# Grouped-query decode attention with adaLN and a small MLP: coarser K turns, 1/L folded into the gather, masks on GpSimd, two more looped V halves, fewer filler matmuls

## The chip, the core and the metric

The kernel runs on one core of one Trainium2 chip. The metric is device time in microseconds (us). The kernel before takes 354.18 us, the median of three runs that lie between 354.14 and 354.19. A profile of one further execution is read throughout. Its engines are PE (TensorE matmuls; PEld is the loading of their weights), DVE (VectorE), ACT (ScalarE), POOL (GpSimd) and SP (SyncE, which here only issues DMAs). A small q behind an engine's name means its sequencer.

## What is computed

One token passes an adaLN block: modulation from a condition vector, a layer norm, attention over a cache of 32768 positions with 8 KV heads and 4 query heads on each, an output projection, a second layer norm and a ReLU MLP.

```python
mod = (_silu(c) @ w_mod).reshape(c.shape[0], 6, 1, -1)
...
h = _layernorm(x, axis=-1) * (1 + ca) + sa
x = x + ga * _A_ref(h, A_k_cache, A_v_cache, A_wq, A_wo)
h = _layernorm(x, axis=-1) * (1 + cb) + sb
x = x + gb * _B_ref(h, B_w1, B_w2)
```

`_A_ref` projects h to q, takes softmax(q·K / sqrt(128))·V for each head and multiplies by `wo`; `_B_ref` is `relu(x @ w1) @ w2`. Everything is bfloat16. K and V of one KV head are 8.39 MB each (32768 x 128), so 134 MB of the 149.4 MB that the kernel reads are the cache.

## The kernel before

**The stream.** SP issues nearly all loads, in one fixed order (the list `stream`, L161 to L168). A load is issued when the code first needs it (`need`, L171), together with everything that stands before it in the list. SP takes its instructions in order: a load that waits holds back all loads behind it. The order is: K of head 0 in two halves with `w_mod` and `wq` between them; then K of head g+1 and V of head g, for g from 0 to 5; then the last head's K mixed with V of head 6; then V of head 7, `wo`, `w1` and `w2`. A whole K or V is one transfer of 8.39 MB. From `HALVED` = 5 on, transfers are halves of 4.19 MB: K6a, K6b, V5a, V5b, K7a, V6a, K7b, V6b, and V7 as one half and two quarters.

**The ring.** All these tiles live in a pool `ring` of three slots of 64 KB per partition. A tile takes the slot of the tile that came three before it, so its first load waits for the last reader of that tile. K6 takes the slot of V3, V5 that of K5, K7 that of V4, V6 that of K6, V7 that of V5, and the tile of the tail weights (`tail_sb`) that of K7.

**One head.** K arrives with 256 positions on each partition, as four tiles u of 64 positions. `turn_k` (L429) lets DVE turn half a tile, 128 x 2048 float32, in place by 32 x 32 blocks. `scores` (L448) multiplies that half with block-diagonal queries (`qbd`, built by ACT in `build_qbd`, L410): 8 matmuls of 512 columns for each half tile, 64 for a head, summed into two PSUM banks. `softmax` (L466) is a generator. Its steps are the maximum (DVE), a transpose of it (PE), the row maximum (DVE), the exponential (ACT, which also sums L), the turn of P (DVE), and 1/L by a matmul and a reciprocal. `pv` (L512) is 64 matmuls of 512 columns for a head, which add four blocks of P·V into 16 PSUM rows. `blocks` (L544) masks and gathers these rows with DVE, `o_cols` turns the result with a matmul, `normalise` (L562) multiplies by 1/L and writes a masked form `oA`, `spread` and `project` (L578, L589) apply `wo`.

**Loops.** `pv` comes in two forms. Unrolled, every matmul names its slice of V. As a loop (L525 to L531) the body of four matmuls stands once, in a section `tc.tile_critical()`, and a register that PE counts up gives the place of the slice in P and in V. Before the section PE waits for everything that was emitted ahead of it, and behind it PE's sequencer counts up a semaphore by which others know that the loop is over. Before the change V0 to V4 and V5b run as loops, the rest unrolled.

**Order.** PE and DVE take the order in which the code emits their work (`manual_schedule`, L633). For each head g the loop at L643 emits: turns and scores of K(g+1), the softmax of head g+1 up to the turn of P, and `pv(g)` within it. For g = 5 `pv(5, (0, 1))`, the use of V5a, stands directly behind the scores of K6 (L655), ahead of that softmax, and V5b behind it (L665). The last two heads are written out from L671 on: turns and scores of K7a, `pv(6, (0, 1))` (L687), turns and scores of K7b, the rest of V6 and V7, then the tail.

**Tail.** Parts of `wo` with index below `WOROWS` are multiplied with the vector as the stationary side (one row of 512 columns a matmul), the others with the weights stationary (four matmuls of one column for each). `keep_clock(n)` (L626) issues n matmuls of 512 columns into a bank that nobody reads.

Of the kernel before, what the change touches and what calls it, by code (L numbers as in the profile page):

```python
# [17 lines left out]
def kernel(  # L18
# [15 lines left out]
    P = 128  # L34
# [12 lines left out]
    WOP = [(0, Hkv // 2), (Hkv // 2, Hkv // 4), (Hkv - 2, 1), (Hkv - 1, 1)]  # L47
    WOROWS = 2
    LAST = Hkv - 1
# [28 lines left out]
    front = ctx.enter_context(tc.tile_pool(name="front", bufs=1))  # L78
    mask4 = front.tile([P, 32], F32, name="mask4_sb")[:, 0:REP]
    ring = ctx.enter_context(tc.tile_pool(name="ring", bufs=3))  # L80
# [124 lines left out]
    nc.vector.tensor_reduce(  # L205
        out=mask4, in_=ident_f[:].rearrange("p (x q) -> p q x", q=REP), op=ALU.add, axis=AX.X,
    )

    cmask, rsel = {}, {}
    for n in sorted({n * REP for _, n in WOP}):  # L210
        cmask[n] = const.tile([P, P // n], F32, name=f"cmask{n}")
        nc.vector.tensor_reduce(
            out=cmask[n][:], in_=ident_f[:].rearrange("p (c r) -> p c r", r=n), op=ALU.add, axis=AX.X,
        )
        rsel_f = const.tile([P, n], F32, name=f"rsel_f{n}")
        nc.vector.tensor_reduce(
            out=rsel_f[:], in_=ident_f[:].rearrange("p (c r) -> p r c", r=n), op=ALU.add, axis=AX.X,
        )
        rsel[n] = const.tile([P, n], BF16, name=f"rsel{n}")
        nc.vector.tensor_copy(out=rsel[n][:], in_=rsel_f[:])  # L220

# [4 lines left out]
    qsel = mask4[0:16, :]  # L226
    oT_sb = const.tile([P, Hq], BF16)
    oA = [const.tile([P, n * REP, P // (n * REP)], BF16, name=f"oA{i}") for i, (_, n) in enumerate(WOP)]
# [31 lines left out]

    acc_ps = ps_acc.tile([P, REP + KT], F32)
    nc.vector.memset(acc_ps[:], 0.0)
    oT_ps, attnT_ps = acc_ps[:, 0:REP], acc_ps[:, REP:REP + KT]

# [63 lines left out]
    for u in range(2):  # L328
        for half in range(2):
            t = need(("k", 0, u))[:, 32 * half:32 * half + 32, :].rearrange("p j d -> p (j d)").bitcast(F32)  # L330
            nc.vector.transpose(out=t, in_=t)  # L331

    mod_b = two_banks("mod_ps")
    mod_ps = [row_bank(mod_b[:, i, :]) for i in range(2)]
    to_rows(mod_ps, siluT, wm_sb, 6)
# [51 lines left out]
    q_b = two_banks("q_ps")  # L387
    q_ps = [row_bank(q_b[:, i, :]) for i in range(2)]
    wq_f = wq_sb.rearrange("p kt (i h a e) -> p kt i a h e", i=2, a=4, e=32)
# [20 lines left out]
    def build_qbd(g):  # L410
        d_ap = qbd[g % 2][:]
        d_ps = d_ap.ap[0][0]
        s_ap = qrep_sb[:]
        s_ps = s_ap.ap[0][0]
        for a in range(4):
            o = AP(d_ap.tensor, d_ap.offset + (32 * a) * d_ps + 4 * 7 + 32 * a,
                   [[d_ps, 32], [QW, 4], [1, 4]])
            i = AP(s_ap.tensor, s_ap.offset + (32 * a) * s_ps + REP * g,
                   [[s_ps, 32], [Hq, 4], [1, 4]])
            nc.scalar.copy(out=o, in_=i)  # L420


    S_tiles, m_tiles, S_ps_tiles = {}, {}, {}
    PT_tiles, Linv_tiles = {}, {}
# [4 lines left out]
    def turn_k(g, u, half):  # L429

        if u == 0 and half == 0:
            S_tiles[g] = two_banks("S_ps")
            m_tiles[g] = spool.tile([P, NG], F32, tag="m2", name="m2")
# [5 lines left out]
        t = nc.vector.transpose(out=KTt.bitcast(F32), in_=KTt.bitcast(F32))  # L439
        behind_loop(t)  # L440
# [21 lines left out]

    def bank_max(g, G):
        behind_loop(nc.vector.reduce_max(out=m_tiles[g][:, G:G + 1], in_=S_tiles[g][:, G, :], axis=AX.X))

    def softmax(g):  # L466

        S_g, m2 = S_tiles.pop(g), m_tiles.pop(g)
        m_p = spool.tile([P, 1], F32, tag="m_p", name="m_p")
        if g < LAST:  # L470
            behind_loop(nc.vector.reduce_max(out=m_p[:], in_=S_g.rearrange("p g f -> p (g f)"), axis=AX.X))  # L471
        else:
            nc.vector.reduce_max(out=m_p[:], in_=m2[:], axis=AX.X)
        yield
# [33 lines left out]
        Linv = spool.tile([P, REP], F32, tag="Linv", name="Linv", bufs=3)  # L508
        nc.vector.reciprocal(out=Linv[:], in_=L_ps[:])  # L509
        Linv_tiles[g] = Linv  # L510

    def pv(g, us, js=range(16)):  # L512

        nb = 4 // len(us)

        PT_g = PT_tiles[g][:].rearrange("p (h j c) -> p h (j c)", h=2, c=32)
        Vs = [need(("v", g, u)) for u in us]

        def step(u, V, PT, Vx):
            nc.tensor.matmul(o_tiles[g][:], lhsT=PT, rhs=Vx, start=False, stop=False, skip_group_check=True)  # L520

        Vf = [V.rearrange("p (s j) d -> p s (j d)", s=4) for V in Vs]
        if g < HALVED or g == HALVED and us[0] > 0:

            with tc.tile_critical() as section:  # L525
                last_loop[:] = loop[:] = [section.name]
                with nc.tensor.Fori(0, 512 - 32 * nb + 1, 32 * nb) as at:
                    for b in range(nb):
                        for u, V in zip(us, Vf):
                            step(u, V, PT_g[:, u // 2, 32 * b + 16 * (u % 2):][:, bass.DynSlice(at, 16)],  # L530
                                 V[:, :, Dh * b:][:, :, bass.DynSlice(at * (Dh // 32), Dh)])  # L531
        else:
            for u, V in zip(us, Vf):
                for j in js:
                    c0 = 32 * j + 16 * (u % 2)
                    step(u, V, PT_g[:, u // 2, c0:c0 + 16], V[:, :, Dh * j:Dh * (j + 1)])

    def open_o(g):
        o_tiles[g] = ps_o.tile([16, 4 * Dh], F32, tag="o", name="o_ps")
        nc.vector.memset(o_tiles[g][:], 0.0)  # L540

    Y_tiles = {}

    def blocks(g):  # L544

        o = o_tiles.pop(g)[:].rearrange("p (s d) -> p s d", s=4)
        Y = spool.tile([16, Dh], F32, tag="Y", name="Y", bufs=1)
        nc.vector.tensor_tensor(  # L548
            out=o, in0=o, in1=smask[:].unsqueeze(2).to_broadcast([16, 4, Dh]), op=ALU.mult,
        )  # L550
# [3 lines left out]
    def o_cols(g):  # L554
        nc.tensor.matmul(  # L555
            oT_ps, lhsT=Y_tiles.pop(g)[:], rhs=qsel, start=True, stop=True, skip_group_check=True,
        )
# [4 lines left out]
    def normalise(g):  # L562
# [3 lines left out]
        CH = P // (n * REP)  # L566
        o_g = oT_sb[:, REP * g:REP * (g + 1)]
        nc.vector.tensor_tensor(out=o_g, in0=oT_ps, in1=Linv_tiles.pop(g)[:], op=ALU.mult)
        nc.vector.tensor_tensor(
            out=oA[i][:, REP * (g - g0):REP * (g - g0 + 1), :],  # L570
            in0=o_g.unsqueeze(2).to_broadcast([P, REP, CH]),
            in1=cmask[n * REP][:].unsqueeze(1).to_broadcast([P, REP, CH]), op=ALU.mult,
        )
        PT_tiles.pop(g)
# [58 lines left out]
    with tc.manual_schedule(engines={mybir.EngineType.PE, mybir.EngineType.DVE}):  # L633
# [189 lines left out]
```

## Time and profile before

| quantity | value |
|---|---|
| time, median of 3 runs | 354.18 us |
| span of the profiled execution, first to last instruction | 352.6 us |
| difference of the two, around the span | 1.6 us |
| PE busy, share of the span | 79% |
| DVE busy | 57% |
| ACT, POOL busy | 7%, 1% |
| matmul instructions | 1310 |
| mean granted clock of TensorE, of full speed | 0.937 |
| bytes moved, mean rate | 149.59 MB, 424 GB/s |

A row of the timeline gives start and length in us, engine, line, operation, what is written and read, the shape and the count; in brackets stands the idle time of the engine before it and what ended it. Consecutive instructions of one line are one row. `SPq ... DMA_DIRECT2D` is the issue of a load, not its transfer. A transfer's landing is seen where an engine's idle time ends by it.

### The profile page before, as it was taken

Reading aid. Unit: us, or ns where it says so; the run is one execution under the profiler, and the core shown is the slowest. Engines: PE = TensorE matmul, PEld = TensorE weight load, DVE = VectorE, ACT = ScalarE, POOL = GpSimd, SP = SyncE. Lnnn points to the kernel's source line nnn. Section 1 sums busy time; section 2 is a strip of 40 time slices with the busy share of each in tenths; the row PEclk is TensorE's granted clock in tenths of the full one; section 3 lists DMA queues with packets and bytes.
Section 4 is the critical chain, followed back from the end, with each engine's and each line's share of the span. In section 5 each row is a group of like instructions: output and inputs, shape, how many; then the busy total and the mean of one; then the engine's idle time right before and its main releaser. Section 6 shows DMA issues by size and latency. Waiting matters only on the chain. (4 is left out here: it accounts for less than half of the span.)

```text
span 352.6 us, 3715 instructions
## 1 busy us (share of the span) xinstructions
PE 277.9 (79%) x1310; PEld 113.5 (32%) x1310; DVE 201.0 (57%) x226; ACT 25.1 (7%) x69; POOL 3.1 (1%) x15
## 2 busy tenths in 40 slices
PE   0065891895998599976998499968999799989994
PEld 0021330331333234322333134323444233434442
DVE  6663564984079614974099506975684257744142
ACT  1200103002000200001000200011000100011000
POOL 2000000000000000000000000000000000000000
PEclk9999897798999879998999879996999989999999
DMA  9999989999999999999999999999999999999995
GB/s 357 398 435 452 472 388 461 454 394 454 461 394 448 439 424 439 424 433 439 416 446 446 409 440 461 411 394 454 431 414 435 457 417 420 444 439 409 425 425 214
DMA packets 5224, 149.59 MB, mean 424 GB/s; under 512 B 604, under 2 KB 988, under 8 KB 1628
## 3 DMA queue, kind: packets, MB, share of 16 engines
q1 hardware_dynamic: 5180, 149.43, 98.5%
q8 instruction: 8, 0.13, 0.1%
q14 instruction: 4, 0.03, 0.0%
q10 hardware_dynamic: 32, 0.00, 0.0%
HBM read 149.42 MB, written 0.00 MB: 424 GB/s over the span
## 5 line engine op out<-in xcount | busy, mean ns | idle before, releaser
L439 DVE STREAM_TRANSPOSE Ksb<-Ksb 128x2048 f32<-128x2048 f32 x60 | 133.1, 2276 | 60.2 <-DMA Ksb<-in_A_k_cache_dram 60.2
L520 PE MATMUL o_ps<-Vsb,P_g 128*16 (+1 forms) x512 | 127.0, 408 | 13.0 <-ACT P_g L495 10.0
L458 PE MATMUL S_ps<-Ksb,qbd 128*128 128x512 bf16 x512 | 120.4, 386 | 10.9 <-DVE Ksb L439 9.3
L458 PEld LDWEIGHTS <-qbd 128*128 128x128 bf16 x512 | 49.6, 98 | 78.1 <-issue 21.8
L520 PEld LDWEIGHTS o_ps<-Vsb,P_g 128*16 x352 | 34.0, 97 | 67.8 <-issue 36.5
L520 PEld LDWEIGHTS <-P_g 128*16 128x16 bf16 x160 | 13.8, 90 | 19.0 <-issue 0.4
L420 ACT COPY qbd<-qrep_sb 32x16 bf16<-32x16 bf16 x32 | 6.4, 201 | 175.2 <-PE S_ps L458 174.1
L500 DVE STREAM_TRANSPOSE P_g<-P_g 128x1024 bf16<-128x1024 bf16 x8 | 10.0, 1245 | 14.1 <-ACT P_g L495 14.1
L471 DVE TENSOR_REDUCE m_p<-S_ps 128x1 f32<-128x1024 f32 x7 | 8.6, 1223 | 13.3 <-PE S_ps L458 13.3
L322 PE MATMUL mod_ps<-wmq_sb,siluT 128*1 128x512 bf16 x24 | 3.6, 624 | 9.9 <-DMA wmq_sb<-in_w_mod_dram 9.9
L331 DVE STREAM_TRANSPOSE Ksb<-Ksb 128x2048 f32<-128x2048 f32 x4 | 8.9, 2280 | 1.6 <-DMA Ksb<-in_A_k_cache_dram 1.6
L476 PE MATMUL mT_ps<-ident_f,m_p 128*1 128x128 f32 x8 | 2.2, 270 | 8.9 <-DVE m_p L471 7.9
L495 ACT ACTIVATE P_g<-S_ps,nbias 128x1024 bf16<-128x1024 f32 x8 | 8.9, 1114 | 0.2
L506 PE MATMUL L_ps<-Lexp,ones_f 128*128 128x4 f32 x16 | 3.1, 263 | 6.3 <-DVE Lexp L503 4.3
L492 ACT ACTIVATE nbias<-Mb_ps 128x1 f32<-128x1 f32 x8 | 1.4, 171 | 88.3 <-PE Mb_ps L490 88.3
L509 DVE RECIPROCAL Linv<-L_ps 128x4 f32<-128x4 f32 x8 | 1.3, 164 | 10.9 <-PE L_ps L506 10.9
L252 PE MATMUL xc_ps<-cx_sel,wmq_sb 16*128 16x2 bf16 x4 | 0.3, 172 | 8.7 <-DVE wmq_sb L246 8.7
L555 PE MATMUL acc_ps<-mask_sb,Y 16*128 16x4 f32 x16 | 3.0, 258 | 4.9 <-DVE Y L551 4.9
L548 DVE TENSOR_TENSOR o_ps<-o_ps,smask 16x512 f32<-16x512 f32 x8 | 5.3, 668 | 2.8 <-PE o_ps L520 2.8
L586 DVE CAST o_sb<-o_ps 128x4 bf16<-128x4 f32 (+2 forms) x4 | 0.7, 165 | 10.3 <-PE o_ps L582 10.3
L506 PEld LDWEIGHTS L_ps<-Lexp,ones_f 128*128 128x128 f32 x16 | 2.6, 203 | 9.6 <-issue 5.6
L551 DVE TENSOR_REDUCE Y<-o_ps 16x128 f32<-16x512 f32 x8 | 5.4, 678 | 0.3
(116 smaller groups left out, 82.8 us busy)
## 6 DMA issues: line engine op xcount, KB each, us to landing
Ksb<-in_A_k_cache_dram SPq DMA_DIRECT2D x5, 4096.0 KB, 23.5
Vsb<-in_A_v_cache_dram SPq DMA_DIRECT2D x5, 4096.0 KB, 38.0
wmq_sb<-in_A_wq_dram SPq DMA_DIRECT2D x1, 4096.0 KB, 28.0
Vsb<-in_A_v_cache_dram SPq DMA_DIRECT2D x2, 2048.0 KB, 38.1
Ksb<-in_A_k_cache_dram SPq DMA_DIRECT2D x1, 4032.0 KB, 37.1
wmq_sb<-in_w_mod_dram SPq DMA_DIRECT2D x1, 3072.0 KB, 18.8
tail_sb<-in_A_wo_dram SPq DMA_DIRECT2D x1, 2048.0 KB, 23.0
tail_sb<-in_B_w_dram SPq DMA_DIRECT2D x1, 1792.0 KB, 30.4
```

Of the source, the lines that this page charges most:

```text
L322: nc.tensor.matmul(dst[j // 4][32 * (j % 4):32 * (j % 4) + 1, :], lhsT=src_T[:, kt:kt + 1], rhs=w[:, kt, j * 512:(j + 1) * 512], start=(kt ...
L331: nc.vector.transpose(out=t, in_=t)
L420: nc.scalar.copy(out=o, in_=i)
L439: t = nc.vector.transpose(out=KTt.bitcast(F32), in_=KTt.bitcast(F32))
L458: nc.tensor.matmul(S_ps_tiles[g], lhsT=qbd[g % 2][:, hp, 4 * (7 - s):4 * (7 - s) + P], rhs=KTv[:, 16 * sl:16 * sl + 16, h, :, par], start= ...
L471: behind_loop(nc.vector.reduce_max(out=m_p[:], in_=S_g.rearrange("p g f -> p (g f)"), axis=AX.X))
L495: nc.scalar.activation(out=P_g[:], in_=S_g.rearrange("p g f -> p (g f)"), func=ACT.Exp, bias=nbias[:], scale=scale, accum_out=l_g[:],)
L500: behind_loop(nc.vector.transpose(out=P_g[:], in_=P_g[:]))
L506: nc.tensor.matmul(L_ps[:], lhsT=ones_f[:], rhs=Lexp[:], start=True, stop=True)
L520: nc.tensor.matmul(o_tiles[g][:], lhsT=PT, rhs=Vx, start=False, stop=False, skip_group_check=True)
L548: nc.vector.tensor_tensor(out=o, in0=o, in1=smask[:].unsqueeze(2).to_broadcast([16, 4, Dh]), op=ALU.mult,)
L551: nc.vector.tensor_reduce(out=Y[:], in_=o.rearrange("p s d -> p d s"), op=ALU.add, axis=AX.X)
```

## The change

The parts, in the order of the program:

- the front builds its masks with fewer instructions, `rsel` is cast by GpSimd, and the two zeroed PSUM banks of `mod_ps` and `q_ps` are one memset each;
- `build_qbd`: one masked GpSimd multiply per head in place of four ACT copies;
- `turn_k`: one turn of a whole tile (128 x 4096 float32) in place of two of half a tile, also for the first half of K0;
- `softmax`: the last head takes its maximum in one pass like the others; L is summed per row block by one matmul with `mask16`, and 1/L is a 16 x 1 column;
- `blocks` multiplies by 1/L while it masks, all heads' columns of o stay in one PSUM tile, and `normalise` writes `oA` once for a part of `wo`;
- `pv`: V5a and V6a become loops, so that with V0 to V4 and V5b eight loops run in place of six; unrolled, head 7's first matmul opens its bank and saves a memset;
- the tail: the third part of `wo` goes with rows (`WOROWS` 3), and 13 of the 18 filler matmuls are gone.

```diff
-    WOROWS = 2
+    WOROWS = 3
...
-    for hp in range(4):
-        h, par = hp // 2, hp % 2
-        src = AP(ib.tensor, ib.offset + 64 * h + par, [[ib.ap[0][0], P], [0, 4], [2, 32]])
-        nc.vector.tensor_copy(out=sel[:, hp, :].rearrange("p (a c) -> p a c", a=4), in_=src)
+    nc.vector.tensor_copy(
+        out=sel.rearrange("p (h par) (a c) -> p h par a c", h=2, a=4),
+        in_=AP(ib.tensor, ib.offset, [ib.ap[0], [64, 2], [1, 2], [0, 4], [2, 32]]),
+    )
...
     def build_qbd(g):
-        for a in range(4):
-            o = AP(d_ap.tensor, d_ap.offset + (32 * a) * d_ps + 4 * 7 + 32 * a,
-                   [[d_ps, 32], [QW, 4], [1, 4]])
...
-            nc.scalar.copy(out=o, in_=i)
+        d_ap, s_ap, m_ap = qbd[g % 2][:], qrep_sb[:], rowpick[:]
+        nc.gpsimd.tensor_tensor(
+            out=AP(d_ap.tensor, d_ap.offset + 4 * 7, [d_ap.ap[0], [QW, 4], [32, 4], [1, 4]]),
+            in0=AP(s_ap.tensor, s_ap.offset + REP * g, [s_ap.ap[0], [Hq, 4], [0, 4], [1, 4]]),
+            in1=AP(m_ap.tensor, m_ap.offset + OUT0, [m_ap.ap[0], [0, 4], [1, 4], [0, 4]]),
+            op=ALU.mult,
+        )
...
     def turn_k(g, u, half):
...
         if g == 0 and u < 2:
             return
+        if half:
+            return
+        KTt = Ksb.rearrange("p j d -> p (j d)")
         t = nc.vector.transpose(out=KTt.bitcast(F32), in_=KTt.bitcast(F32))
         behind_loop(t)
...
-        Lexp = spool.tile([P, REP], F32, tag="Lexp", name="Lexp")
-        nc.vector.tensor_scalar(out=Lexp[:], in0=mask4, scalar1=l_g[:], scalar2=None, op0=ALU.mult)
         yield
-        L_ps = small_ps([P, REP], "L_ps")
-        nc.tensor.matmul(L_ps[:], lhsT=ones_f[:], rhs=Lexp[:], start=True, stop=True)
+        L_ps = small_ps([16, 1], "L_ps")
+        nc.tensor.matmul(L_ps[:], lhsT=mask16, rhs=l_g[:], start=True, stop=True)
...
+    def looped(g, us):
+        return g <= HALVED or g == LOOPED and us == (0, 1)
+
     def pv(g, us, js=range(16)):
...
-        if g < HALVED or g == HALVED and us[0] > 0:
+        if looped(g, us):
...
     def blocks(g):
...
-        nc.vector.tensor_tensor(
-            out=o, in0=o, in1=smask[:].unsqueeze(2).to_broadcast([16, 4, Dh]), op=ALU.mult,
+        nc.vector.scalar_tensor_tensor(
+            out=o, in0=o, scalar=Linv_tiles.pop(g)[:], in1=smask[:].unsqueeze(2).to_broadcast([16, 4, Dh]),
+            op0=ALU.mult, op1=ALU.mult,
         )
...
     def normalise(g):
...
-        nc.vector.tensor_tensor(out=o_g, in0=oT_ps, in1=Linv_tiles.pop(g)[:], op=ALU.mult)
...
+        if g == g0 + n - 1:
+            nc.vector.tensor_tensor(
+                out=oA[i][:], in0=oT_ps[:, REP * g0:REP * (g0 + n)].unsqueeze(2).to_broadcast([P, n * REP, CH]),
+                in1=cmask[n * REP][:].unsqueeze(1).to_broadcast([P, n * REP, CH]), op=ALU.mult,
+            )
...
-        bank_max(h, 0)
         pv(g, (0, 1))
...
-        bank_max(h, 1)
         soft = softmax(h)
...
         project(0)
-        keep_clock(2)
         o_cols(LAST)
-        keep_clock(2)
         project(1)
         normalise(LAST)
         spread(3)
-        keep_clock(2)
         project(2)
-        keep_clock(1)
         join_rows()
         keep_clock(1)
         project(3)
...
-            keep_clock(2)
             x1_ps.append(four_rows(e, "x1"))
             keep_clock(2)
 
-        keep_clock(3)
         layernorm_T(x1T[:], stat2, h2T[:], modT_sb[:, 3 * KT:4 * KT], ncb[:], "ln2", meanwhile)
...
-        keep_clock(3)
+        keep_clock(2)
```

In the built program the loads keep their order. Two of them have a new wait: the second halves of V5 and of V6 now stand behind the end of the loop that reads the first half (counts 18 and 24 of the semaphore that PE's sequencer raises by 3 for each loop). The place of a loop's slice lies in a register, so the planner takes the loop to read all of its V tile, and both halves are written to one tile.

More of the change, by code (lines that the diff above doesn't have):

```diff
@@ L78 @@
     front = ctx.enter_context(tc.tile_pool(name="front", bufs=1))
-    mask4 = front.tile([P, 32], F32, name="mask4_sb")[:, 0:REP]
+    mask16 = front.tile([P, 32], F32, name="mask16_sb")[:, 0:16]
+    mask4 = mask16[:, 0:REP]
     ring = ctx.enter_context(tc.tile_pool(name="ring", bufs=3))
@@ L205 @@
     nc.vector.tensor_reduce(
-        out=mask4, in_=ident_f[:].rearrange("p (x q) -> p q x", q=REP), op=ALU.add, axis=AX.X,
+        out=mask16.rearrange("p (s q) -> p s q", q=REP),
+        in_=AP(ident_f[:].tensor, ident_f[:].offset, [ident_f[:].ap[0], [0, 4], [1, REP], [REP, P // REP]]),
+        op=ALU.add, axis=AX.X,
     )
@@ L219 @@
         rsel[n] = const.tile([P, n], BF16, name=f"rsel{n}")
-        nc.vector.tensor_copy(out=rsel[n][:], in_=rsel_f[:])
+        nc.gpsimd.tensor_copy(out=rsel[n][:], in_=rsel_f[:])
     smask = const.tile([16, 4], F32)
@@ L258 @@
     cT, xT = xc[:, 0, :], xc[:, 1, :]
-    acc_ps = ps_acc.tile([P, REP + KT], F32)
+    acc_ps = ps_acc.tile([P, Hq + KT], F32)
     nc.vector.memset(acc_ps[:], 0.0)
-    oT_ps, attnT_ps = acc_ps[:, 0:REP], acc_ps[:, REP:REP + KT]
+    oT_ps, attnT_ps = acc_ps[:, 0:Hq], acc_ps[:, Hq:Hq + KT]
     def bank(name):
@@ L328 @@
     for u in range(2):
-        for half in range(2):
-            t = need(("k", 0, u))[:, 32 * half:32 * half + 32, :].rearrange("p j d -> p (j d)").bitcast(F32)
-            nc.vector.transpose(out=t, in_=t)
+        t = need(("k", 0, u)).rearrange("p j d -> p (j d)").bitcast(F32)
+        nc.vector.transpose(out=t, in_=t)
     mod_b = two_banks("mod_ps")
-    mod_ps = [row_bank(mod_b[:, i, :]) for i in range(2)]
+    row_bank(mod_b)
+    mod_ps = [mod_b[:, i, :] for i in range(2)]
     to_rows(mod_ps, siluT, wm_sb, 6)
@@ L387 @@
     q_b = two_banks("q_ps")
-    q_ps = [row_bank(q_b[:, i, :]) for i in range(2)]
+    row_bank(q_b)
+    q_ps = [q_b[:, i, :] for i in range(2)]
     wq_f = wq_sb.rearrange("p kt (i h a e) -> p kt i a h e", i=2, a=4, e=32)
@@ L410, in build_qbd @@
     def build_qbd(g):
[L411 to L414, printed above, removed]
-        for a in range(4):
-            o = AP(d_ap.tensor, d_ap.offset + (32 * a) * d_ps + 4 * 7 + 32 * a,
-                   [[d_ps, 32], [QW, 4], [1, 4]])
[L418 to L423, printed above, removed]
+        d_ap, s_ap, m_ap = qbd[g % 2][:], qrep_sb[:], rowpick[:]
[5 more added lines that the diff above has]
+        )
+    S_tiles, S_ps_tiles = {}, {}
     PT_tiles, Linv_tiles = {}, {}
@@ L517, in pv, with step @@
         Vs = [need(("v", g, u)) for u in us]
-        def step(u, V, PT, Vx):
-            nc.tensor.matmul(o_tiles[g][:], lhsT=PT, rhs=Vx, start=False, stop=False, skip_group_check=True)
+        def step(u, V, PT, Vx, first=False):
+            nc.tensor.matmul(o_tiles[g][:], lhsT=PT, rhs=Vx, start=first, stop=False, skip_group_check=True)
         Vf = [V.rearrange("p (s j) d -> p s (j d)", s=4) for V in Vs]
-        if g < HALVED or g == HALVED and us[0] > 0:
+        if looped(g, us):
             with tc.tile_critical() as section:
@@ L555, in o_cols @@
         nc.tensor.matmul(
-            oT_ps, lhsT=Y_tiles.pop(g)[:], rhs=qsel, start=True, stop=True, skip_group_check=True,
+            oT_ps[:, REP * g:REP * (g + 1)], lhsT=Y_tiles.pop(g)[:], rhs=qsel,
+            start=True, stop=True, skip_group_check=True,
         )
```

24 lines of the change are left out of this document (6 added, 18 removed).

## The prediction

> **What bounds the kernel now.** I read the page first, then the chain of waits in order of time, then the timeline of SP alone.
>
> ```profile
> span 352.6 us, 3715 instructions
> PE 277.9 (79%) x1310; PEld 113.5 (32%) x1310; DVE 201.0 (57%) x226; ACT 25.1 (7%) x69; POOL 3.1 (1%) x15
> ...
> DMA  9999989999999999999999999999999999999995
> ...
> q1 hardware_dynamic: 5180, 149.43, 98.5%
> q8 instruction: 8, 0.13, 0.1%
> q14 instruction: 4, 0.03, 0.0%
> ```
>
> No engine is full, but SP's queue keeps the 16 DMA engines busy for 98.5% of the span, and the DMA row shows no slice below 8 tenths except the last. The load stream bounds the kernel: work on an engine counts only if it makes a load late, or lies behind the last load. The chain ends that way:
>
> ```profile
> 313.39 25.04 DMA tail_sb<-in_A_wo_dram
> 338.42 0.02 issue
> 338.44 11.14 DMA tail_sb<-in_B_w_dram
> 349.58 0.04 issue
> 349.62 0.29 PE end_ps L784 x4
> ```
>
> The last load ends at 349.58, and 3.0 us follow it. So the question for each edit is whether it opens a gap in the stream. The reserve is the distance from the issue of a load to the landing of the load ahead of it. The issues around the change, and the landings that DVE waited for:
>
> ```profile
> 234.34 0.81 SPq L154 DMA_DIRECT2D Vsb<-in_A_v_cache_dram  x2
> 256.12 0.33 SPq L154 DMA_DIRECT2D Ksb<-in_A_k_cache_dram  x1
> 270.62 0.33 SPq L154 DMA_DIRECT2D Vsb<-in_A_v_cache_dram  x1
> 270.99 0.43 SPq L154 DMA_DIRECT2D Ksb<-in_A_k_cache_dram  x1
> 271.46 19.78 SPq L154 DMA_DIRECT2D Vsb<-in_A_v_cache_dram  x4
> ...
> 313.02 1.75 SPq L154 DMA_DIRECT2D tail_sb<-in_A_wo_dram  x4
> ```
>
> ```profile
> 243.75 8.89 DVE L439 STREAM_TRANSPOSE Ksb<-Ksb 128x2048 f32<-128x2048 f32 x4 [2.73 <-DMA Ksb<-in_A_k_cache_dram]
> ...
> 282.51 4.51 DVE L439 STREAM_TRANSPOSE Ksb<-Ksb 128x2048 f32<-128x2048 f32 x2 [0.46 <-DMA Ksb<-in_A_k_cache_dram]
> ...
> 302.15 8.89 DVE L439 STREAM_TRANSPOSE Ksb<-Ksb 128x2048 f32<-128x2048 f32 x4 [2.70 <-DMA Ksb<-in_A_k_cache_dram]
> ```
>
> K6a lands at 243.75 and K7a at 282.51, four half transfers later: 38.76 / 4 = 9.69 us each. Hence K6b lands at 253.4, V5a at 263.1, V5b at 272.8, V6a at 292.2, K7b at 302.1, V6b at 311.8. V5a and V5b are issued together at 234.34, K7a at 256.12, V6a and K7b at 270.6 to 271.0. The load ahead of K7a, V5b, lands 16.7 us after K7a's issue: a delay of a few us anywhere costs nothing, as long as loads are issued in pairs like this.
>
> **The change part by part: the loops.** V5b now waits until the loop on V5a is over. That loop cannot start before V5a has landed, at 263.1, and SP issues in order, so K7a, V6a and K7b wait behind V5b. When V5a has landed, nothing is queued. The gap lasts until PE has come to the loop, has run it, SP has issued V5b and its transfer has started.
>
> ```profile
> 238.86 0.19 ACT L495 ACTIVATION_READ_ACCUMULATOR P_g<-S_ps,nbias 128x1 f32 x1
> 239.65 16.31 PE L520 MATMUL o_ps<-Vsb,P_g 128*16 x64 [2.04 <-ACT P_g L495]
> ...
> 256.51 14.07 PE L458 MATMUL S_ps<-Ksb,qbd 128*128 128x512 bf16 x64
> ...
> 270.53 7.07 PE L520 MATMUL o_ps<-Vsb,P_g 128*16 128x512 bf16 x32
> ...
> 280.74 9.03 PE L520 MATMUL o_ps<-Vsb,P_g 128*16 x32 [2.10 <-DMA Ksb<-in_A_k_cache_dram]
> ```
>
> The scores of K6 keep PE until 256.51 + 14.07 = 270.58, whatever V5a does. The entry into a section takes 0.6 us: ACT's sum is there at 239.05, and the loop on V4 starts at 239.65. Unrolled, 32 matmuls take 7.07 us; I take this for the loop too, since PE comes hot from the scores (the upper end is the 9.03 us of the loop on V5b, which started after an idle stretch). SP's issue follows a loop's end closely: the loop on V4 ends at 255.96, K7a is issued at 256.12, 0.16 us later.
>
> What is a load worth that meets an empty queue? The trace has one, the first:
>
> ```profile
> 0.74 0.38 SPq L154 DMA_DIRECT2D Ksb<-in_A_k_cache_dram  x1
> ...
> 12.76 8.89 DVE L331 STREAM_TRANSPOSE Ksb<-Ksb 128x2048 f32<-128x2048 f32 x4 [1.63 <-DMA Ksb<-in_A_k_cache_dram]
> ```
>
> A half of the same size needs 12.0 us from issue to use. The ends are 9.69 us (no start-up at all) and 12.0 us; I take 12.0, the only row with an empty queue. The Trainium skill (DMA: Bandwidth & Descriptors, Anatomy of one DMA) gives a fixed 2.0 us plus bytes over 436 GB/s, fitted on the other issue path; an estimate from it for 4.19 MB is 11.6 us, and by it each gap below would be 0.4 us shorter, the total 376.4.
>
> **The turns of K** move the start of that loop. A whole tile turns in the time of its halves, but PE gets nothing of it before the end.
>
> ```profile
> 223.51 8.85 DVE L439 STREAM_TRANSPOSE Ksb<-Ksb 128x2048 f32<-128x2048 f32 x4
> ...
> 232.41 1.90 PE L458 MATMUL S_ps<-Ksb,qbd 128*128 128x512 bf16 x8 [0.30 <-DVE Ksb L439]
> ```
>
> ```profile
> L439 DVE STREAM_TRANSPOSE Ksb<-Ksb 128x2048 f32<-128x2048 f32 x60 | 133.1, 2276 | 60.2 <-DMA Ksb<-in_A_k_cache_dram 60.2
> ...
> L500 DVE STREAM_TRANSPOSE P_g<-P_g 128x1024 bf16<-128x1024 bf16 x8 | 10.0, 1245 | 14.1 <-ACT P_g L495 14.1
> ```
>
> In K5 the scores run right behind DVE: 8 matmuls follow the last half turn. With whole tiles 16 follow it, 8 x 0.22 = 1.8 us more. Against that four fixed parts of a turn go: by the two shapes one instruction costs 214 ns plus 1.007 ns a column, and successive turns start 2.21 us apart, 0.07 less than one lasts, so at most 0.15 us each. The shift lies between +1.2 and +1.8; I take +1.5. It passes on through the softmax of head 5, the loop on V4 and the scores of K6, which follow each other on PE without slack. K6b's own turns (ready by then) stay covered by the scores of K6a.
>
> **First gap.** Scores of K6 end at 270.6 + 1.5 = 272.1; entry 0.6, loop 7.07: 279.8; issue 0.16: 280.0; landing 280.0 + 12.0 = 292.0 in place of 272.8. That is **+19.2 us**.
>
> **Second gap.** K7a, V6a and K7b are issued right behind V5b and land at 301.7, 311.4 and 321.1. V6b must wait for the loop on V6a; without a gap it would land at 330.8.
>
> ```profile
> 290.60 4.47 DVE L439 STREAM_TRANSPOSE Ksb<-Ksb 128x2048 f32<-128x2048 f32 x2
> 295.00 0.65 DVE L548 TENSOR_TENSOR o_ps<-o_ps,smask 16x512 f32<-16x512 f32 x1
> 295.67 0.68 DVE L551 TENSOR_REDUCE Y<-o_ps 16x128 f32<-16x512 f32 x1
> 296.41 0.38 PE L555 MATMUL acc_ps<-mask_sb,Y 16*128 16x4 f32 x2 [0.71 <-DVE Y L551]
> 296.72 1.92 PE L458 MATMUL S_ps<-Ksb,qbd 128*128 128x512 bf16 x8
> ```
>
> The loop on V5b runs from 292.6 for 9.0 us and ends at 301.6. K7a's two tiles are turned by 301.7 + 2 x 4.45 + 0.2 (a reciprocal) = 310.8. Then PE does 8 scores, the gathered o of head 5, 8 scores and a spread: about 4.1 us, to 314.9; entry 0.6, loop 7.07: 322.6; issue: 322.7; landing 334.7, **+3.9 us**. If a load starts without start-up this is 1.6; if the loop runs 9.03 us it is 5.9.
>
> ```profile
> 280.00:286.00 6.00, 5.15 (x16) 1.87 (x17) 5.33 (x5) 0.08 (x1) 0.00 (x0) 0.72 1.01 437
> ```
>
> After 2.1 us of idling the granted clock in this stretch is 0.72. In the second gap PE idles some 4.5 us ahead of K7a's first scores. The Trainium skill (TensorE: Matmul & The Clock Gate, Part 1) says that an idle window of about 3.4 us halves the clock, and a busy one restores it; by it those 16 matmuls take 1.7 us more and the second gap grows by at most 0.6 us, since the second turn covers the rest. The trace agrees in kind.
>
> After that nothing new is late: the loop on V5b freed V7's slot, so V7 follows V6b at once, and the tail weights need only the scores of K7b, which end near 333.4 while the queue is filled until V7 has landed near 354.
>
> **The tail and the rest.**
>
> ```profile
> 345.30 0.93 PE L761 MATMUL hid_ps<-tail_sb,h2T 128*1 128x448 bf16 x16 [1.28 <-DMA tail_sb<-in_B_w_dram]
> ...
> L631 PE MATMUL spare_ps<-qbd,ident_bf 128*128 128x512 bf16 x18 | 5.4, 381 | 0.0
> L420 ACT COPY qbd<-qrep_sb 32x16 bf16<-32x16 bf16 x32 | 6.4, 201 | 175.2 <-PE S_ps L458 174.1
> ```
>
> Thirteen fillers less leave PE with holes. The attention result is needed when `w1` lands, and PE stood idle for 1.28 us there, so the reordered projection (the turn of the rows now comes after part 2, about 0.3 us later) stays hidden. If the clock fell to half, the 16 matmuls behind `w1` and those behind `w2` would take up to 1.3 us more at the end; I take 0 and keep 1.3 for the range. Query masks on POOL are 8 instructions in place of 32 copies of 0.2 us; whether one costs 0.1 or 2 us, they run a head ahead of their use, and the first only delays loads that are queued far ahead. One multiply less per head on DVE, 1/L in the gather, the masks in front: all lie beside the stream and cost or save nothing there. A shorter program saves at most the two instruction queues' 0.1% of the span, 0.35 us.
>
> **Sum.** 19.2 + 3.9 = 23.1 us on the profiled span of 352.6 gives 375.7. The runs' median stands 1.6 us above that span, so 354.18 + 23.1 = **377.3 us**. Low end: 16.6 (the first gap with 2.3 less for the start-up and 0.3 less for the turns) + 1.6 - 0.35 = 17.9: 372.1. High end: 19.5 + 5.9 + 1.3: 380.9.
>
> **The rivals.**
> - Only the first gap opens, because PE reaches the loop on V6a early enough that V6b is queued before K7b has landed. That needs 3.9 us less between V5b's landing and that loop's end. For it: a faster start of loads. Against: turns of 4.45 us stand in that path. 354.18 + 19.2 = 373.4. Chance 0.11.
> - The mark that V5b waits for is set when the loop is entered. Then V5b is issued at 272.7 and lands at 284.7, +11.9, and V6b is in time: 366.1. Against it: K7a's issue at 256.12, right at the end of the loop on V4 and not at its start. Chance 0.05.
> - The transfer is hidden anyway, the other side: V5b would have to be issued about 2 us (12.0 less 9.69) before V5a lands, by 261, for the stream not to notice. Then only the shorter program and the tail are left, -0.35 to +0.3 us, about 354.1. For it: every issue in the trace before has such a lead. Against: a loop that reads V5a would have to end before V5a is there. That is also the case in which the change does only what its list says. Chance 0.04.
> - Both gaps open and PE runs cold through both loops and the tail: above 381. Chance 0.03.
>
> **How the numbers follow.** Both gaps: 0.77, with 372.1 to 380.9 from the bounds above. The likeliest time is 377.3. I round the range to 371.5 to 381.5, which takes in the first rival and leaves out about 0.12. A measurement of this kernel can tell about 0.2%, 0.7 us, from no change. Faster by more: 0.01 and within: 0.03 (both from the third rival). Slower by more: 0.96, all the rest.
>
> **What would show it.** In the profile after: the issue of V5b alone, near 280, behind the end of the first loop on V5, and three loads right behind it; a slice or two of the DMA row near 265 to 281 that fall to nearly nothing; landings of K7a near 301.7 and K7b near 321; a second, short hole near 322; the stream unbroken from there, with the same 3 us behind its last load. SP's waits for PE's sequencer should grow by some 45 us, since it stands at V5b from 236 on. If the DMA row stays at 9 near 265, the main step is wrong; if the holes are there but shorter, a start-up or the entry of a loop was mis-sized.

## The result, and the profile after

The changed kernel takes 382.27 us, the median of four runs between 381.89 and 382.72, beside 354.19 (354.14 to 354.38) for the kernel before: a ratio of 1.0791, 95% interval 1.0775 to 1.0807. It is slower by 28.1 us; 377.3 was predicted, with 371.5 to 381.5 as range. The profiled execution has a span of 380.1 us, 27.5 more than before. Some executions of a kernel took several per cent longer at random; all times and ratios here and below are of the others.

The page of the changed kernel:

```profile
span 380.1 us, 3704 instructions
...
PE 280.7 (74%) x1285; PEld 113.0 (30%) x1285; DVE 196.3 (52%) x163; ACT 18.7 (5%) x37; POOL 6.0 (2%) x26
...
DMA  8999999999999999999999999994039997799994
...
q1 hardware_dynamic: 5180, 149.43, 91.6%
...
L415 POOL TENSOR_TENSOR qbd<-qrep_sb,rowpick 128x64 bf16<-128x64 bf16 x8 | 2.3, 298 | 227.8 <-PE S_ps L460 198.0
```

The same bytes by the same packets, but the queue is busy for 91.6% of a longer span in place of 98.5%. The DMA row has two holes: one around slices 28 to 30, one around 34 and 35. PE is busy for 280.7 us in place of 277.9 and DVE for 196.3 in place of 201.0, so the added time is no added work of theirs. The stretches of time (length, busy time and instructions by engine, then granted clock, DMA share, GB/s) and SP's timeline show the holes and what stands in them:

```profile
260.00:264.00 4.00, 4.00 (x20) 1.76 (x19) 4.00 (x2) 0.00 (x0) 0.00 (x0) 1.00 0.27 111
264.00:268.00 4.00, 4.00 (x21) 1.74 (x19) 3.12 (x1) 0.00 (x0) 0.00 (x0) 1.00 0.00 0
...
276.00:280.00 4.00, 4.00 (x17) 1.35 (x16) 0.00 (x0) 0.00 (x0) 0.00 (x0) 1.00 0.00 0
280.00:284.00 4.00, 1.84 (x9) 0.85 (x8) 0.67 (x3) 1.38 (x3) 0.00 (x0) 1.00 0.47 147
...
308.00:312.00 4.00, 4.00 (x12) 1.40 (x11) 4.00 (x2) 0.00 (x0) 0.00 (x0) 0.58 1.06 459
...
316.00:320.00 4.00, 3.34 (x16) 1.23 (x15) 0.17 (x1) 0.00 (x0) 0.00 (x0) 1.00 0.91 393
```

```profile
235.76 45.78 SPq L155 DMA_DIRECT2D Vsb<-in_A_v_cache_dram  x2
281.59 0.42 SPq L155 DMA_DIRECT2D Ksb<-in_A_k_cache_dram  x1
282.18 0.33 SPq L155 DMA_DIRECT2D Vsb<-in_A_v_cache_dram  x1
282.55 0.53 SPq L155 DMA_DIRECT2D Ksb<-in_A_k_cache_dram  x1
325.66 1.86 SPq L155 DMA_DIRECT2D Vsb<-in_A_v_cache_dram  x4
```

V5a is issued at 235.76, V5b at the end of that row, near 281.2, and the three loads behind it within 1.5 us: SP stood at V5b and held them back. V6b follows alone at 325.66. SP's own waits (total, times, longest) have it too, first before, then after:

```profile
SPq L154 <- PEq L525: 124.9, 6, 21.9
```

```profile
SPq L155 <- PEq L522: 173.6, 6, 45.1
```

PE and DVE around these issues:

```profile
273.02 8.03 PE L517 MATMUL o_ps<-Vsb,P_g 128*16 x32 [0.73 <-issue]
...
294.64 8.73 PE L517 MATMUL o_ps<-Vsb,P_g 128*16 x32 [12.29 <-issue]
...
307.52 7.06 PE L460 MATMUL S_ps<-Ksb,qbd 128*128 128x512 bf16 x24 [3.62 <-DVE Ksb L441]
...
317.40 8.06 PE L517 MATMUL o_ps<-Vsb,P_g 128*16 x32 [0.66 <-issue]
```

```profile
303.02 4.45 DVE L441 STREAM_TRANSPOSE Ksb<-Ksb 128x4096 f32<-128x4096 f32 x1 [17.39 <-DMA Ksb<-in_A_k_cache_dram]
307.39 0.11 DVE L503 RECIPROCAL Linv<-L_ps 16x1 f32<-16x1 f32 x1
307.44 4.41 DVE L441 STREAM_TRANSPOSE Ksb<-Ksb 128x4096 f32<-128x4096 f32 x1
...
322.27 8.77 DVE L441 STREAM_TRANSPOSE Ksb<-Ksb 128x4096 f32<-128x4096 f32 x2 [5.32 <-DMA Ksb<-in_A_k_cache_dram]
```

The loop on V5a ends at 281.05, and V5b's issue follows. K7a lands at 303.02 in place of 282.51: the first gap is **20.5 us**. K7b lands at 322.27; with V6b queued behind it, V6b would land 9.69 later, at 331.96. The chain of waits, which ends last, has its landing:

```profile
325.66 13.35 DMA Vsb<-in_A_v_cache_dram
339.02 0.02 issue
339.03 33.41 DMA tail_sb<-in_B_w_dram
372.44 0.14 issue
372.58 1.66 PE hid_ps L751 x13
```

V6b is there at 339.0: the second gap is **7.1 us**. 20.5 + 7.1 = 27.6, and the span grew by 27.5. So two late loads account for the whole of it in this profile; what remains is which edits they come from and why both are larger than forecast.

### The profile page after: what moved, and what is told of

It reads as the page before. It is cut to its first block, busy times and chain, and to the rows that moved or that the text cites. A ratio compares the mean times of both kernels' runs of the same rounds, so it can differ in the third digit from the quotient of the medians.

```text
span 380.1 us, 3704 instructions
## 1 busy us (share of the span) xinstructions
PE 280.7 (74%) x1285; PEld 113.0 (30%) x1285; DVE 196.3 (52%) x163; ACT 18.7 (5%) x37; POOL 6.0 (2%) x26
## 3 DMA queue, kind: packets, MB, share of 16 engines
q1 hardware_dynamic: 5180, 149.43, 91.6%
## 5 line engine op out<-in xcount | busy, mean ns | idle before, releaser
L441 DVE STREAM_TRANSPOSE Ksb<-Ksb 128x4096 f32<-128x4096 f32 x30 | 131.2, 4415 | 72.6 <-DMA Ksb<-in_A_k_cache_dram 72.6
L517 PE MATMUL o_ps<-Vsb,P_g 128*16 (+1 forms) x512 | 130.0, 410 | 28.1 <-issue 13.7
L460 PE MATMUL S_ps<-Ksb,qbd 128*128 128x512 bf16 x512 | 121.8, 393 | 20.2 <-DVE Ksb L441 19.2
L517 PEld LDWEIGHTS o_ps<-Vsb,P_g 128*16 x416 | 39.3, 94 | 89.4 <-issue 55.3
L469 DVE TENSOR_REDUCE m_p<-S_ps 128x1 f32<-128x1024 f32 x8 | 9.8, 1224 | 26.6 <-PE S_ps L460 26.6
L517 PEld LDWEIGHTS <-P_g 128*16 128x16 bf16 x96 | 8.5, 92 | 15.5 <-DMA Vsb<-in_A_v_cache_dram 2.9
L332 DVE STREAM_TRANSPOSE Ksb<-Ksb 128x4096 f32<-128x4096 f32 x2 | 8.8, 4424 | 1.6 <-DMA Ksb<-in_A_k_cache_dram 1.6
L546 DVE SCALAR_TENSOR_TENSOR o_ps<-o_ps,Linv,smask 16x512 f32<-16x512 f32 x8 | 5.8, 720 | 2.8 <-PE o_ps L517 2.8
L475 DVE TENSOR_REDUCE Mrow<-mT_ps 1x4 f32<-1x128 f32 x8 | 2.2, 273 | 7.6 <-PE mT_ps L472 7.6
L415 POOL TENSOR_TENSOR qbd<-qrep_sb,rowpick 128x64 bf16<-128x64 bf16 x8 | 2.3, 298 | 227.8 <-PE S_ps L460 198.0
L568 DVE TENSOR_TENSOR oA<-acc_ps,cmask 128x128 bf16<-128x128 f32 x4 | 1.2, 292 | 8.5 <-PE acc_ps L554 8.5
## 6 DMA issues: line engine op xcount, KB each, us to landing
wmq_sb<-in_A_wq_dram SPq DMA_DIRECT2D x1, 4096.0 KB, 28.1
```

What stands on the lines that cost most here:

```text
L460: nc.tensor.matmul(S_ps_tiles[g], lhsT=qbd[g % 2][:, hp, 4 * (7 - s):4 * (7 - s) + P], rhs=KTv[:, 16 * sl:16 * sl + 16, h, :, par], start= ...
L517: nc.tensor.matmul(o_tiles[g][:], lhsT=PT, rhs=Vx, start=first, stop=False, skip_group_check=True)
L546: nc.vector.scalar_tensor_tensor(out=o, in0=o, scalar=Linv_tiles.pop(g)[:], in1=smask[:].unsqueeze(2).to_broadcast([16, 4, Dh]), op0=ALU.m ...
```

## The experiments

Each edit is against the changed kernel unless said otherwise. All times are medians, beside runs of the kernel before on the same chip (354.3 to 354.4).

**The loops taken back.** Only the condition for a loop is as before:

```diff
-        return g <= HALVED or g == LOOPED and us == (0, 1)
+        return g < HALVED or g == HALVED and us[0] > 0
```

> The changed kernel, but with the first halves of V5 and V6 unrolled again, as before; every other edit stays (whole-tile turns, masks by GpSimd, 1/L in the gather, fewer fillers). Late loads (theory): V5b and V6b are issued with V5a and V6a again, both gaps close, 353.9 to 354.6 us, SP's wait for PE's sequencer falls from 173.6 back to about 125 us, and the DMA row shows no slice below 8 tenths before the last. The other edits carry it (rival): whole-tile turns and colder PE alone cost most of the 28 us, so it stays above 375. A mixture would show in between: the turns shift K5's scores by 1.4 us, and if that reached the end it would be 355.6.

Measured: 354.35 us, ratio 0.9997 (0.9988 to 1.0007). SP's wait for PE's sequencer is back at 124.6 us. Without the two loops, all other edits together cost and save nothing that can be measured.

**The loops alone**, in the kernel before:

```diff
-        if g < HALVED or g == HALVED and us[0] > 0:
+        if g <= HALVED or g == LOOPED and us == (0, 1):
```

> The kernel before with one edit of the change: V5a and V6a run as loops. Late loads: both gaps open. In the changed kernel they were worth 20.5 (V5b landing at 293.3 in place of 272.8) and 7.1 (V6b landing at 339.0 in place of 332.0 had it followed K7b). Without whole-tile turns K5's scores end 1.4 us earlier, and K7a's scores follow its half turns more closely, so the first gap is 19.1, the second 5 to 7: 378 to 381 us. The other edits carry it: 354 to 356.

Measured: 379.91 us, ratio 1.0722 (1.0707 to 1.0738). K7a lands at 301.48, a first gap of 19.0 us, K7b at 321.65, and PE's first matmul on V6b starts at 337.18, 5.8 us after 321.65 + 9.69. One edit of the list makes 25.5 of the 28.1 us, and with the run above the main cause is settled. The other 2.4 us (382.27 less 379.91) come from the other edits, but only beside the loops.

**One half at a time.** First V5a's loop without V6a's, then V6a's without V5a's:

```diff
-        return g <= HALVED or g == LOOPED and us == (0, 1)
+        return g <= HALVED
```

```diff
-        return g <= HALVED or g == LOOPED and us == (0, 1)
+        return g < HALVED or g == HALVED and us[0] > 0 or g == LOOPED and us == (0, 1)
```

> The changed kernel with V5a as a loop and V6a unrolled as before. Late loads: the first gap alone, 20.5 us; V6b is queued with V6a again, and nothing opens behind it: 354.2 + 20.5 = 374.7 us (373.8 to 375.6). Loops are slow in themselves (rival: what costs is PE's time in the loops and in the code around them, not a late load): half of the 28 us, about 368.

> The changed kernel with V6a as a loop and V5a unrolled as before. Late loads: V5b is queued in time, so K7a, V6a and K7b land near 282.5, 292.2 and 301.9 as before. K7a's turns and scores end near 296, the loop on V6a runs from about 297 for 8.03 us to 305, V6b is issued at 305.2 and lands 12.0 to 13.4 us later, at 317.2 to 318.6, in place of 311.8: a gap of 5.4 to 6.8, 359.6 to 361.0 us. Loops are slow in themselves: again half of the 28 us, about 368. If the second gap exists only because the first has made the queue short (rival), it stays at 354 to 355.

Measured: 376.75 us (ratio 1.0626) with V5a alone; 364.78 us (1.0292) with V6a alone. Each loop opens its own gap, so the rival that the second gap needs the first falls; they cost 22.3 and 10.4 us, not half of the 28 each, so the rival of loops that are slow in themselves falls too. Both expectations were too low, V5a's by 1 to 3 us (some 1 us of it is the tail, below; the rest was not followed up), V6a's by 4 to 5. From the latter kernel's timelines of DVE, PE and SP:

```profile
283.94 4.40 DVE L441 STREAM_TRANSPOSE Ksb<-Ksb 128x4096 f32<-128x4096 f32 x1
...
292.23 4.42 DVE L441 STREAM_TRANSPOSE Ksb<-Ksb 128x4096 f32<-128x4096 f32 x1
...
301.81 8.77 DVE L441 STREAM_TRANSPOSE Ksb<-Ksb 128x4096 f32<-128x4096 f32 x2 [0.84 <-DMA Ksb<-in_A_k_cache_dram]
```

```profile
301.42 8.08 PE L517 MATMUL o_ps<-Vsb,P_g 128*16 x32 [0.66 <-issue]
...
322.23 2.73 PE L517 MATMUL o_ps<-Vsb,P_g 128*16 128x512 bf16 x6 [3.85 <-DMA Vsb<-in_A_v_cache_dram]
```

```profile
309.67 2.18 SPq L155 DMA_DIRECT2D Vsb<-in_A_v_cache_dram  x4
```

I had let K7a's second turn follow the first, from 288.3. It stands behind the loop on V5b and starts at 292.23, so the loop on V6a starts at 301.42 and not at 297. V6b lands at 322.2, 10.7 us after 301.81 + 9.69. The two costs add up to 32.7 us and not to 28.1: with the first gap PE runs the loop on V5b as soon as V5b lands (294.64, landing 293.3); without it PE is 10 us behind (282.83, landing some 273), and so further behind the loads when V6a's turn comes.

**The load issued ahead of the loop.** The loops stay; the second half's load is asked for first:

```diff
+        if looped(g, us) and us == (0, 1):
+            need(("v", g, 2))
```

> The changed kernel, with one line more: where a half of V runs as a loop over tiles 0 and 1, the load of tiles 2 and 3 is issued ahead of that loop. The loops stay as they are; the loop on V5a now waits for V5b too, and the loop on V6a for V6b. Late loads (theory): the stream has no hole, SP's wait for PE's sequencer falls by some 45 us, and the time is that of the kernel before, 354 to 356 us (the upper end, because the loop on V6a now starts only when V6b has landed, near 312, and K7b's scores stand behind it). Loops are slow in themselves, or a loop on a half stops other work (rival): it stays at 368 to 382 us.

Measured: 369.65 us, ratio 1.0424 (1.0402 to 1.0446). The stream is whole, as expected (SP waits 126.9 us for PE's sequencer), but only 12.6 of the 28 us come back. The page's DMA row and PE's timeline of this kernel (its L519 is L517 of the changed one):

```profile
DMA  8999999999999999999999999999999999989910
```

```profile
312.89 9.27 PE L519 MATMUL o_ps<-Vsb,P_g 128*16 x32 [10.39 <-issue]
322.35 7.11 PE L460 MATMUL S_ps<-Ksb,qbd 128*128 128x512 bf16 x32 [0.19 <-PEq L524]
...
360.21 1.66 PE L753 MATMUL hid_ps<-tail_sb,h2T 128*1 128x448 bf16 x16
```

The stream now has its hole at the end: all loads are there while PE still works. The loop on V6a starts 10.4 us late. The profile names no releaser, but the loop now stands behind V6b's load, and in the unbroken stream of the kernel before V6b lands near 311.8. K7b's scores, the uses of V6b and V7 stand behind it on PE, which from there to the matmuls on `w1` (360.21) waits for no load. The late load has become a late engine. To see which half does it, the same two lines with only one of the loops, by the conditions of the two kernels before:

> The changed kernel with V5a as a loop and V5b's load issued ahead of that loop; V6a unrolled as before. With both halves ahead the load stream had no hole, and yet it took 369.65 us: the loop on V6a waited for V6b, 10.4 us, and K7b's scores behind it. Theory: that wait alone is what was left, a loop on V5a whose next load is already queued costs nothing, and the time is 354.3 to 355.0 us. Loops on halves cost PE time that ends up in the end (rival): half of the 15.3 us, about 362, since then each of the two loops has its share.

> The changed kernel with V5a unrolled as before, V6a as a loop, and V6b's load issued ahead of that loop. Theory: the stream stays whole, PE's work behind V6b sets the end, as with both halves ahead: 368.8 to 370.4 us, and the last load lands some 10 us ahead of the end of PE's work. Rival (each loop has its share): about 362.

Measured: 369.64 us with V6a's loop alone, as with both, so V6a's wait is what was left. With V5a's loop alone it is 357.17 us (ratio 1.0076, 1.0059 to 1.0093), 2.8 us over the kernel before, not 0 to 0.7. Two rows each of PE's timeline, first of the kernel with all loops as before, then of this one:

```profile
272.02 7.07 PE L517 MATMUL o_ps<-Vsb,P_g 128*16 128x512 bf16 x32
...
345.58 1.66 PE L751 MATMUL hid_ps<-tail_sb,h2T 128*1 128x448 bf16 x16
```

```profile
274.36 8.04 PE L519 MATMUL o_ps<-Vsb,P_g 128*16 x32 [2.22 <-DVE o_ps L548]
...
348.06 1.66 PE L753 MATMUL hid_ps<-tail_sb,h2T 128*1 128x448 bf16 x16
```

A section waits for all that was emitted ahead of it, here for V5b too, so it starts 2.3 us later. The matmuls behind `w1`, 74 us on, start 2.5 us later, and the span is 355.3 in place of 352.6. In neither kernel do they wait for `w1` (no bracket); in the kernel before they waited 1.28 us. In the first of these two kernels the chain of waits already runs through PE and DVE from 291 us on, not through the loads. PE is a second bound, so close behind the stream that a delay of 2.5 us comes out whole.

**The length of a loop's body.** Why 8.03 us for 32 matmuls that take 7.07 unrolled? The weight loads of the loop on V5a in the changed kernel, four rows of eight:

```profile
273.01 0.54 PEld L517 LDWEIGHTS o_ps<-Vsb,P_g 128*16 x4 [1.02 <-issue]
273.99 0.59 PEld L517 LDWEIGHTS o_ps<-Vsb,P_g 128*16 x4 [0.43 <-issue]
275.01 0.54 PEld L517 LDWEIGHTS o_ps<-Vsb,P_g 128*16 x4 [0.43 <-issue]
...
280.01 0.54 PEld L517 LDWEIGHTS o_ps<-Vsb,P_g 128*16 x4 [0.43 <-issue]
```

One round of four starts every 1.00 us, and nothing that the profile shows is waited for; four matmuls at full clock take 4 x 0.22 = 0.88 (7.07 us for 32). So the round seems to be set by what feeds PE, and a longer body tests that. (In the loop on V0 of the trace before, and in that on V5b with both loads ahead, rounds of 1.09 to 1.12 us stand; why they differ is open.) The trace before has rounds of 1.00 us at the end of its loop on V2:

```profile
174.48 0.54 PEld L520 LDWEIGHTS o_ps<-Vsb,P_g 128*16 x4 [0.34 <-issue]
175.46 0.58 PEld L520 LDWEIGHTS o_ps<-Vsb,P_g 128*16 x4 [0.43 <-issue]
```

The edit makes the body eight matmuls long:

```diff
-        nb = 4 // len(us)
+        nb = 8 // len(us)
```

> The changed kernel with twice as many matmuls in each loop body (8 in place of 4 for the halves, 8 in place of 4 for the whole heads) and half as many rounds. The loops on V5a and V6a took 8.03 and 8.06 us where 32 unrolled matmuls take 7.07. If the excess is a cost of each round (registers, branch), about half of it goes in each: loops of 7.5 us, each gap 0.5 us shorter, and the loop on V4 ahead of them shorter as well by up to 1 us: 380.1 to 381.4 us. If it is a cost of each matmul with a register in its address (rival), the loops keep 8.0 us and the time stays at 382.3. If it is the code that has to be brought in (rival), the longer bodies cost more: above 382.5.

Measured: 379.31 us, 3.0 us less than the changed kernel (ratio to before 1.0698, 1.0680 to 1.0716). PE's timeline of this kernel:

```profile
273.26 7.07 PE L517 MATMUL o_ps<-Vsb,P_g 128*16 x32 [0.68 <-issue]
...
316.76 7.07 PE L517 MATMUL o_ps<-Vsb,P_g 128*16 x32 [0.67 <-issue]
```

Both loops fall to the unrolled 7.07 us: all of the excess goes, not half of it, so it is a cost of the round that a longer body hides. That makes 2.0 us, all of the difference between the two profiled executions (381.89 and 379.92); the first is the fastest of its four runs and the second the slowest of its four, which makes up the 3.0 between the medians. The same edit on the kernel with V5a's loop and its load ahead tests the second bound:

> V5a as a loop with V5b's load ahead of it, V6a unrolled, and 8 matmuls in each loop body. With 4 it took 357.17 us, 2.7 us more, though the load stream was whole. Theory: from the scores of K6 on PE has no idle time, so it is a second bound behind the stream; the loop's entry (274.36 in place of 272.02, since it waits for V5b) and its longer run (8.04 in place of 7.07) come out at the end. With the longer body the run falls by 1.0 us and with it the time, to 356.0 to 356.4 us. Rival: the 2.7 us lie in the loads, and the body changes nothing: 357.0 to 357.4.

Measured: 354.85 us (ratio 1.0026, 1.0009 to 1.0043; runs from 354.10 to 356.66), 2.3 less, more than expected. There the loop on V5b falls as well, from 8.97 to 7.09 us, which I had not counted. A part of that is the clock: from 284 to 292 us it was granted at 0.78 to 0.79 with the short body and at 1.00 with the long one. With both loads ahead the loop on V5b had four matmuls and a clock of 1.00, and took 8.73. The profile is of the fastest of the eight runs:

```profile
274.01 7.07 PE L519 MATMUL o_ps<-Vsb,P_g 128*16 x32 [2.49 <-DVE o_ps L548]
...
283.46 7.09 PE L519 MATMUL o_ps<-Vsb,P_g 128*16 x32 [1.08 <-ACT nbias L488]
...
345.02 1.66 PE L753 MATMUL hid_ps<-tail_sb,h2T 128*1 128x448 bf16 x16 [0.50 <-DMA tail_sb<-in_B_w_dram]
```

PE's work on `w1` moves from 348.06 to 345.02 and waits for `w1` again: in this execution the stream bounds once more. The wait for V5b still costs PE nearly 2 us, but the shorter loops pay for it. The slower executions were not profiled.

**Half turns of K**, as before (three lines removed):

```diff
-        if half:
-            return
-        KTt = Ksb.rearrange("p j d -> p (j d)")
```

> The changed kernel with K turned half a tile at a time, as before; everything else of the change stays. Turns shift the scores (theory): K5's scores end 1.4 us earlier, so the first gap is 19.0 us in place of 20.5, and the second about 5.8 in place of 7.0, as in the kernel before with the loops alone: 354.3 + 24.8 = 379.1 us, up to 380.0 where the tail's colder PE adds its part. Turns cost nothing (rival): 382.3 us.

Measured: 381.35 us (runs 379.18 to 381.62), 0.9 less than the changed kernel by the medians; the expectation was 1.4 to 2.3 too low. The profile is of the slowest run. K7a lands at 302.08, so the first gap shrank by 0.9. The second did not shrink: V6b's first matmul is at 338.35, 7.0 us after 321.63 + 9.69. There the last eight scores of K7a took 3.18 us:

```profile
312.43 0.38 PE L551 MATMUL acc_ps<-mask_sb,Y 16*128 16x4 f32 x2 [1.65 <-DVE Y L547]
312.75 3.18 PE L457 MATMUL S_ps<-Ksb,qbd 128*128 128x512 bf16 x8
```

and the stretch around them, in the view by stretches:

```profile
312.00:316.00 4.00, 3.50 (x11) 1.35 (x11) 0.70 (x3) 0.00 (x0) 0.00 (x0) 0.65 1.17 492
```

The granted clock was 0.65 there; with the loops alone it was 1.00 at the same place, and they took 1.91. Half turns leave PE short holes, and between these two profiles it differed whether the clock falls in them. It may also differ from run to run of one kernel: the run of 379.18 us, which is in the expected range, had a mean granted clock of 0.914, the three others 0.892 to 0.901. No profile of it shows where.

**The fillers of the tail**, put back; first with V5a's loop (without its load ahead), then with all loops as before. Their places are those of the diff of the change:

```diff
         project(0)
+        keep_clock(2)
         o_cols(LAST)
+        keep_clock(2)
         project(1)
...
```

> The changed kernel with V5a as a loop, V6a unrolled, and the 18 fillers of before in the tail. Without those fillers it took 376.75 us, 22.3 more than before, where its first gap accounts for 20.1 (K7a landed at 302.58 in place of 282.51). In its tail the 16 matmuls behind w1 took 1.66 us in place of 0.93, and those behind w2 2.93. Cold tail (theory): with the fillers these fall back, the time falls by 0.7 to 1.9 us, to 374.9 to 376.1. Rest of the 2.2 us lies in the loads (rival): 376.5 to 377.

> The changed kernel with the first halves of V5 and V6 unrolled, as before, and the 18 fillers of before in the tail. Without the fillers it took 354.44 us, and PE went from the loops to the 16 matmuls behind w1 without a wait; those took 1.66 us, at half clock. Theory: PE's tail and the last load end within half a us of each other there, so a warm tail gives back at most that: 353.8 to 354.4 us. Rival: the fillers stand in PE's way, since it has no idle time there: 354.6 to 355.5.

Measured: 375.62 us in place of 376.75 with V5a's loop, in the expected range. The runs overlap (375.54 to 376.17, and 375.77 to 377.07), but the trace shows 0.7 us of the gain: the 16 matmuls behind `w1` take 0.93 us in place of 1.66. With the loops as before 354.18 us (ratio 0.9998, 0.9989 to 1.0007) in place of 354.35 (354.44 in the expectation): no difference that these runs can tell. Neither this nor any other version beats the kernel before by more than 0.2%.

## Why the prediction was right, and where it was not

- **The bound and the mechanism: right.** V5b is issued behind the end of the loop on V5a with three loads at its heels, the DMA row falls to 0, SP's wait grows by 48.7 us (some 45 forecast), a second hole opens before V6b. None of the rivals came: V6a's loop does not reach its end in time, V5b is not issued at the loop's entry, the transfer is not hidden. The time is that of the fourth rival, above 381, but not by its cause: both loops on the first halves ran at full clock (1.00 from 276 to 280 and from 316 to 320).
- **The loop on a half: the step that failed.** "Unrolled, 32 matmuls take 7.07 us; I take this for the loop too, since PE comes hot from the scores." It took 8.03 and 8.06 us. Being hot (at full clock) was no reason for the short value but for the long one: when PE runs at half clock (a matmul every 0.43 us, 1.7 for four) it is slower than what feeds it, and only a hot PE waits for the round of 1.00 us. The trace before shows such rounds too, at the end of the loop on V2; I had read the loop on V4 alone. The term stands in both gaps, +1.0 each. These 2.0 us are the largest part of the 4.5 by which the two gaps were forecast too short; V6b's start-up (1.35), the way from K7a's second turn to the loop on V6a (0.85) and the entry of the first loop (0.3) are most of the rest. With the loop's term right the forecast would have been 379.3, still 3.0 short. Moreover I used the upper value of 9.03 only for the second gap; in both it would have put the high end near 383, and the result inside.
- **First gap, 19.2 forecast, 20.5 measured.** +1.0 from the loop, +0.3 from its entry and the scores ahead of it (273.02 in place of 272.7). Start-up: 281.2 to 303.02 - 9.69 = 293.3 is 12.1 us, forecast 12.0. An estimate from the formula of the Trainium skill (DMA: Bandwidth & Descriptors, Anatomy of one DMA), which was fitted on GpSimd's path, is 11.6; the trace has 12.1 for SP's, and decides. (By 11.6 in both gaps the prediction's sum is 376.5, not the 376.4 that it gives.)
- **Second gap, 3.9 forecast, 7.1 measured.** From K7a's landing to V6b's it is 36.0 us in place of 33.0: the loop +1.0; V6b's start-up 13.35 in place of 12.0; from the end of the second turn (311.85) to the loop 5.55 in place of 4.7; the turns themselves 0.3 less. Of the third, 0.8 is the clock: where PE stayed hot (V6a's loop alone) that stretch took 4.77 (296.65 to 301.42). The Trainium skill (TensorE: Matmul & The Clock Gate, Part 1) says that an idle window of about 3.4 us halves the clock. The trace agrees: after 3.62 us of idling the granted clock was 0.58 (308 to 312). But it was also 0.50 from 240 to 244, behind three idle times of 1.10 to 1.99 us, so shorter holes can do it too. The price of the 3.62 us, 0.8, was a little over the 0.6 that I allowed.
- **The start-up of V6b stays open.** V5b needed 12.1 us, V6b 13.35 here and 12.5 with V6a's loop alone. No run tells why.
- **The turns of K: right at their place, smaller at the end.** K5's scores end 1.4 us later (1.5 forecast); half turns gave back 0.9 in all by the medians.
- **The tail and the rest: right.** The two gaps make 27.6 of 27.5 us, so the tail cost nothing here, though the chain ends with PE at half clock (1.66 us behind `w1` in place of 0.93). The upper bound of 1.3 had its reason: with V5a's loop alone the fillers were worth about 1.1. Masks by GpSimd (8 multiplies of 298 ns each by the page), 1/L in the gather and the shorter program: nothing, 0.9997 with the loops as before.
- **"Work on an engine counts only if it makes a load late, or lies behind the last load": incomplete.** It held for the changed kernel, whose gaps gave PE time. With the gaps closed PE is a second bound, 1.28 us behind the stream before the change. That 1.28 stood in the prediction as cover for one projection; it was the whole slack of PE.

## What to carry to other kernels

Where a section's end is what frees a buffer or lets a load be issued, the next load of an in-order queue has to be issued ahead of the section. To leave no gap it must be issued before the load ahead of it lands, by at least its start-up (2.4 us here: 12.1 us from issue to landing less the 9.69 us that one transfer takes); but then see what the section itself now waits for, and what stands behind it. When a queue is 98% busy, look at the idle time in front of the last loads for the distance of the next bound before calling work hidden. A loop's body should run longer on the engine than its round takes to feed (here four matmuls, 0.88 us, did not, and eight, 1.77 us, did), and that is to be read from rounds that run hot.

## What was not expected of the hardware

- A loop of four matmuls of 512 columns with places taken from a register runs at one round in 1.00 us, where PE needs 0.88 at full clock; with eight in the body the 32 matmuls take 7.07 us, as unrolled. After the idle stretch of the first gap, where the clock starts low, no gain of the longer body can be seen: 8.98 us for V5b, where the loops of four took 8.73 to 9.91 in the five kernels with that gap.
- PE's clock did not follow from the order of the work alone: the same eight scores, behind holes of nearly the same length (1.58 and 1.65 us), took 1.91 us in one profile and 3.18 in another.
